# Output copies and the single tokens' first splits in the second MLP of a fused attention and MLP kernel

## The chip, the cores and the metric

The kernel runs on one core of one Trainium2 chip. The metric is the device time of one launch in microseconds (us). Before the change it is 966.17 us, the median of three runs that lie between 964.99 and 968.43 us. TensorE (PE) multiplies matrices, VectorE (DVE) and ScalarE (ACT) do elementwise work, GpSimd (POOL) hardly works here, and SyncE (SP) issues the DMAs.

## What is computed

A windowed attention with global tokens gives 2304 tokens of 512 features. They go through a gated MLP (512 to 1536 to 512) and then through a second MLP (512 to 2048 to 512) with a leaky ReLU. The change touches the second MLP alone.

```python
x = np.ascontiguousarray(attn_out.transpose(0, 2, 1, 3)).reshape(B * S, H * D)   # 2304 x 512
x = _moe_ref(x=x, **moe_kwargs)          # first MLP, 512 -> 1536 -> 512
h = x @ w_in                             # second MLP, 512 -> 2048
g = np.maximum(0.01 * h, h)
out = (g @ w_out).astype(np.float32)     # 2048 -> 512
```

All of it is float32. Each operand of a matrix product is split into a high part in the fast format fp32r (a cast on ACT, `high`, line 82) and a low part, the rest (a subtraction on DVE, `low`, line 85). A product is then three matmuls (`mm3`, line 78): high by high, one operand's low by the other's high, and the reverse. So a matmul has to wait for ACT's cast and then for DVE's subtraction.

## The kernel before

The attention runs ahead of and beside the first MLP. The second MLP follows as a section of its own at the end (functions `up`, `dn`, `out_tile` and the `rest_` functions, and one loop over g that calls them). Its order is written out by hand: on PE, DVE, ACT and SP each engine does its work in the order in which the code is written, so an instruction that waits holds up everything behind it on its engine.

The 2304 tokens of the second MLP are two blocks of 1024 tokens (s = 0 and 1) and 128 single tokens (REST). A block goes through 16 steps, numbered g: eight steps `up` (j = 0 to 7) make the hidden values, a pair of 128-wide columns each, and eight steps `dn` multiply them by `w_out`. So g = 0 to 7 and 8 to 15 are block 0, g = 16 to 23 and 24 to 31 block 1. PAIRS is 8.

- `up(g)` forms its hidden values from seven products of sums of blocks instead of eight (the tokens' sums are `ysa` and `ysb`, the weights' sums `wr`). PE's products in order are px, pw, py, pz into four PSUM banks, then a second px, py and pz on top of the first. Between a bank's two products the first result is read: ACT copies px into `x1`, DVE adds `u2 = x1 + pw`, `v = u2 + py`, `h[3] = v + pz`. Only then may PE add the second py onto py (line 1084) and the second pz onto pz. `x1`, `u2` and `v` are three SBUF buffers of 128 by 512, one each, and every step takes the same three again.
- The hidden values of pair j lie in a buffer of its own with tag `h0` to `h7`, 128 by 4 by 512. `dn` splits them into high and low (`dop_of`), four pieces a pair, some steps ahead.
- The weights' sums `wr` of block 0 are made in the kernel (`make_w` with place 0, 1 and 2, one step ahead: two casts on ACT of 128x768 and 128x1024, two subtractions on DVE of the same shapes, and at place 2 also the load of a later pair's weights, `load_q`). They are stored in DRAM by `keep_parts`, and block 1 loads them from there (`fetch_w`, line 929, 1792 KB each). There are two `wr` buffers, so the load for a step can start when PE has done the step before last.
- The single tokens are worked through beside the 16 `up` steps, two units a step: `rest_pair(u)` splits the weights of two units on ACT and DVE and issues the loads of the next two (two `raw` buffers, line 984), `rest_step(u)` is a unit's three matmuls (pr for the first layer, po for the second). Before the first of them `rest_second` splits the tokens themselves (`yr`). In step 0 these come at the end of `up`, in later steps earlier.
- In the last `dn` step of a block (j = 7) PE finishes the eight output tiles one after the other, six matmuls each. `out_tile` copies a tile from PSUM to an SBUF buffer `ob` (DVE and ACT in turn) and SP stores it to DRAM (line 973). The buffers are those of `x1`, `u2` and `v`, tile t in the place t modulo 3.

Of the kernel before, what the change touches and what calls it, by code (L numbers as in the profile page):

```python
# [8 lines left out]
F32 = mybir.dt.float32  # L9
# [7 lines left out]
P = 128  # L17
# [7 lines left out]
def tile_window_global_attention_two_mlps(  # L25
# [12 lines left out]
    _, _, KB, NT, _ = v_b.shape  # L38
# [6 lines left out]
    DM = NP * P  # L45
# [35 lines left out]
    def high(hi, src):  # L81
        nc.scalar.copy(hi, src)  # L82

    def low(lo, src, hi):
        nc.vector.tensor_tensor(out=lo, in0=src, in1=hi.bitcast(F32), op=ALU.subtract)  # L85

    def split(hi, lo, src):
        high(hi, src)
        low(lo, src, hi)
# [44 lines left out]
    def bank(name, early=False):  # L134

        return pools[0].tile([P, 512], F32, tag="y" if early else "b", bufs=pools[1], name=name)
# [486 lines left out]
    PAIRS = NF2 // 2  # L623
# [43 lines left out]
    def weight_sums(q):  # L667

        a21, a22, a11, a12, s1, s2, s3, s4 = (q[:, s] for s in range(8))
        for dst, x, y, op in ((s1, a21, a22, ALU.add), (s2, s1, a11, ALU.subtract),  # L670
                              (s3, a11, a21, ALU.subtract), (s4, a12, s2, ALU.subtract)):
            nc.vector.tensor_tensor(out=dst, in0=x, in1=y, op=op)
# [5 lines left out]
    def weight_parts(j):  # L678

        t = w_in[0, j] = ring(j)  # L680
        return [(t[:, 0, r], t[:, 1, r], slice(r.start + 1, r.stop + 1)) for r in (slice(0, 3), slice(3, 7))]

    def keep_parts(j):
        nc.sync.dma_start(out=w2_dram[j], in_=w_in[0, j].bitcast(F32).rearrange("p y s c -> p y (s c)"))
# [4 lines left out]
    def load_q(j):  # L689

        if j < PAIRS:
            q = wq[j] = quarter() if j % 2 else rings[1].tile([P, 8, HK], F32, tag=f"h{PAIRS - 1}", name=f"q{j}")
            for s, f in ((0, j + PAIRS), (2, j)):
                nc.sync.dma_start(out=q[:, s:s + 2].rearrange("p s c -> p (s c)"), in_=w2_f32[f][0])
# [203 lines left out]
    wp2 = ctx.enter_context(tc.tile_pool(name="wp2", bufs=1, reuse_waits="tile"))  # L898
# [13 lines left out]
    def kind(g):  # L912
        s, r = divmod(g, 2 * PAIRS)
        return (s, *divmod(r, PAIRS))

    def fetch_w(g):

        if g >= NU:
            return
        s, layer, j = kind(g)  # L920
        if layer:
            t = ring(g).rearrange("p y s c -> p (y s c)")
            raw = wfs[g] = t[:, 4 * DM:6 * DM].bitcast(F32).rearrange("p (f c) -> p f c", f=2)
            w_out[g] = t[:, 0:4 * DM].rearrange("p (y f c) -> p y f c", y=2, f=2)
            for x, f in enumerate((j, j + PAIRS)):
                nc.sync.dma_start(out=raw[:, x], in_=w2_f32[f][1])
        elif s:
            t = w_in[s, j] = ring(g)
            nc.sync.dma_start(out=t.bitcast(F32).rearrange("p y s c -> p y (s c)"), in_=w2_dram[j])

    def make_w(g, place):

        if g >= NU:
            return
        s, layer, j = kind(g)
        if layer:
            if place == 0:
                high(w_out[g][:, 0], wfs[g])
            elif place == 1:
                low(w_out[g][:, 1], wfs[g], w_out[g][:, 0])  # L940
        elif s == 0:
            q = wq[j]
            if place == 0:
                wq["parts"] = weight_parts(j)
                high(wq["parts"][0][0], q[:, wq["parts"][0][2]])
                weight_sums(q)
            elif place == 1:
                low(wq["parts"][0][1], q[:, wq["parts"][0][2]], wq["parts"][0][0])
                high(wq["parts"][1][0], q[:, wq["parts"][1][2]])
            else:  # L950
                low(wq["parts"][1][1], q[:, wq["parts"][1][2]], wq["parts"][1][0])
                load_q(j + 2)
# [5 lines left out]
    def product(s, j, which, dst, start=True):  # L958
        w, part, x = PRODUCT[which]
        t, y = w_in[s, j], ys2[s, part]  # L960
        for k in range(KC // 2):
            mm3(dst, [t[:, h, w, k * P:(k + 1) * P] for h in range(2)], [y[:, h, k, x] for h in range(2)],
                start and k == 0, k == KC // 2 - 1, not start)

    def plus(out, x, y):
        nc.vector.tensor_tensor(out=out, in0=x, in1=y, op=ALU.add)

    def leaky(out, x):
        nc.scalar.activation(out=out, in_=x, func=AF.Prelu, alpha=0.01)

    def store_rows(c0, ob):
        for r0, o, m in rows(c0, P):
            nc.sync.dma_start(out=out[r0:r0 + m, :], in_=ob[o:o + m, :])
# [5 lines left out]
    def rest_load(u):  # L979

        raw = rest["raw", u] = wp2.tile([P, HALF], F32, tag="raw", bufs=2, name=f"raw{u}")
        if u < NRU:
            fq, kc = divmod(u, KC)
            nc.sync.dma_start(out=raw.rearrange("p (f c) -> p f c", c=P), in_=w2_fours[fq][:, :, kc * P:(kc + 1) * P])
        else:
            nc.sync.dma_start(out=raw, in_=w2_f32[u - NRU][1])

    def rest_split(u):

        t = rest["w", u] = halves_tile(f"rw{u}")  # L990
        split(t[:, 0], t[:, 1], rest.pop(("raw", u)))
        if u >= NRU and u % 4 == 0:
            t = rest["h"] = wp2.tile([P, 2, 4, P], F32R, tag="yr", name=f"hr{u}")
            split(t[:, 0], t[:, 1], rest["hid"][:, u - NRU:u - NRU + 4])

    def rest_pair(u):
        for x in (u, u + 1):
            rest_split(x)
        for x in (u + 2, u + 3):
            if x < NRU + NF2:  # L1000
                rest_load(x)

    def rest_first():
        rest["y32"] = wp2.tile([P, HALF], F32, tag="hn", name="yr32")
        nc.sync.dma_start(out=rest["y32"].rearrange("p (k c) -> p k c", k=KC), in_=y_dram[:, :, 0:REST])

    def rest_second():
        rest["y"] = wp2.tile([P, 2, KC, P], F32R, tag="yr", name="yr")
        split(*(rest["y"][:, h].rearrange("p k c -> p (k c)") for h in range(2)), rest["y32"])
        rest["hid"] = wp2.tile([P, NF2, P], F32, tag="hid", name="hid")  # L1010
# [33 lines left out]
    def dop_of(s, x):  # L1044

        if x < 4 * PAIRS:
            j, r = divmod(x, 4)
            f, n = SLOTS[r]
            t = dops[s, x] = halves_tile(f"d{s}_{x}")
            split(t[:, 0], t[:, 1], hid[s, j][:, 2 * n + f])  # L1050

    def up(g):
        s, _, j = kind(g)
        u = 2 * (s * PAIRS + j)
        if g == 0:
            rest_first()
            rest_load(0)
            rest_load(1)
            load_q(2)
        if (s, j) != (1, 0):  # L1060
            fetch_w(g + 1)
        if s == 0 and j:
            keep_parts(j)
        h = hid[s, j] = wp2.tile([P, 4, HALF], F32, tag=f"h{j}", name=f"h{s}_{j}")
        x1, u2, v = [wp2.tile([P, HALF], F32, tag=x, name=f"{x}{s}_{j}") for x in ("x1", "u2", "v")]
        bx, bw, by = [bank(f"p{c}{s}_{j}") for c in "xwy"]
        product(s, j, 1, bx)
        nc.scalar.copy(x1, bx)
        product(s, j, 6, bw)
        plus(u2, x1, bw)  # L1070
        if g:
            rest_pair(u)
        product(s, j, 7, by)
        plus(v, u2, by)
        make_w(g + 1, 0)
        bz = bank(f"pz{s}_{j}")
        product(s, j, 5, bz)
        plus(h[:, 3], v, bz)
        make_w(g + 1, 1)
        product(s, j, 2, bx, False)  # L1080
        leaky(h[:, 0], bx)
        if j == PAIRS - 1:
            dop_of(s, 0)
            dop_of(s, 1)
        product(s, j, 4, by, False)
        plus(h[:, 1], u2, by)
        make_w(g + 1, 2)
        if g:
            rest_step(u)
        product(s, j, 3, bz, False)  # L1090
        plus(h[:, 2], u2, bz)
        leaky(h[:, 1:4], h[:, 1:4])
        if j == PAIRS - 1:
            dop_of(s, 2)
        if not g:
            rest_second()
            rest_pair(u)
            rest_step(u)
        rest_step(u + 1)

    def out_tile(s, t, last):
        ob = wp2.tile([P, DM], F32, tag=("x1", "u2", "v")[t % 3], name=f"ob{s}_{t}")
        if last % 2:
            nc.vector.tensor_copy(ob, dn.op[t])
        else:
            nc.scalar.copy(ob, dn.op[t])
        store_rows(REST + 2 * HALF * s + t * P, ob)
# [102 lines left out]
```

## Time and profile before

| | before |
|---|---|
| median of three runs | 966.17 us (964.99 to 968.43) |
| the profiled execution, its own time | 969.37 us |
| its span, first to last instruction | 967.6 us |
| granted TensorE clock, mean (1 is 2.4 GHz) | 0.985 |
| busy: PE, DVE, ACT | 927.2 us (96%), 585.6 us (61%), 461.1 us (48%) |
| chain that ended last, by engine | PE 72%, DMA 7%, DVE 3%, ACT 2% |
| of it, DMA of `ob` to the output | 2% |

The busy share of an engine is a mean over all stages. The chain that ended last is followed back from the last instruction, at each step to what released it, and so shows which waits count. The timeline gives each instruction with its start, its duration and, in brackets, how long its engine stood idle before it and what ended that. In the second MLP, from about 597 us on, PE is busy nearly without a gap but in two places, near 608 us and near 788 us.

### The profile page before, as it was taken

The numbers are of one execution on the slowest core, as the hardware profiler recorded it, in microseconds if no ns is written. First come the engines' busy times: TensorE is split into PE (matmuls) and PEld (weight loads), VectorE is DVE, ScalarE is ACT, GpSimd is POOL, SyncE is SP. The second block draws the span as 40 slices with busy tenths as digits, with TensorE's granted clock in tenths as the row PEclk, the third lists the DMA queues.
The fourth block names the chain that finished last, engine by engine and source line by source line (L and its number), as shares of the span: only waits on it lengthen the run. The fifth ranks groups of instructions, "written<-read, shape, count | busy, mean of one in ns | idle before, by whom it ended". The sixth has DMA issues, their size and how long they took to land.

```text
span 967.6 us, 14064 instructions
## 1 busy us (share of the span) xinstructions
PE 927.2 (96%) x5056; PEld 759.4 (78%) x5056; DVE 585.6 (61%) x1216; ACT 461.1 (48%) x958; POOL 4.5 (0%) x26
## 2 busy tenths in 40 slices
PE   6799999999999999999999999899999969999998
PEld 4557777777777777777899999688888858888886
DVE  5689985597676887444577744577665224445332
ACT  6886774655554555333454422445544213434331
POOL 1000000000000000000000000000000000000000
PEclk9899999999999999999999999999999979999999
DMA  9588994886769999744789982576333355651113
GB/s 305 172 284 264 313 354 150 273 286 226 253 215 380 346 367 343 260 131 142 283 282 338 362 296 79 200 276 246 142 93 104 94 188 196 225 189 54 44 47 107
DMA packets 87174, 215.37 MB, mean 223 GB/s; under 512 B 11456, under 2 KB 25280, under 8 KB 85056
## 3 DMA queue, kind: packets, MB, share of 16 engines
q1 hardware_dynamic: 87104, 214.47, 64.3%
q8 instruction: 40, 0.66, 0.3%
q14 instruction: 30, 0.25, 0.1%
HBM read 154.14 MB, written 60.29 MB: 222 GB/s over the span
## 4 chain that ended last, share of the span: by engine, by line
PE 72%; DMA 7%; DVE 3%; ACT 2%; issue 1%; SPq 0%; DVEq 0%; ACTq 0%
PE o L78 17%; PE pg L78 10%; PE yp L78 10%; PE pv L78 10%; PE py L78 5%; PE px L78 4%; PE pz L78 4%; DMA q<-y_dram 2%; PE pw L78 2%; PE po L146 2%; DMA out<-ob 2%; PE sc L146 2%; DMA y_dram<-ys 2%; PE pp L255 1%; PE pr L78 1%; PE po L78 1%
## 5 line engine op out<-in xcount | busy, mean ns | idle before, releaser
L78 PE MATMUL o<-wr,d 128*128 128x512 f32 x768 | 174.4, 390 | 0.0
L78 PEld LDWEIGHTS o<-wr,d 128*128 128x128 f32 x768 | 144.3, 188 | 29.8
L78 PE MATMUL pg<-xh,w 128*128 128x512 f32 (+1 forms) x464 | 132.6, 368 | 0.4 <-ACT xh L82 0.4
L78 PE MATMUL pv<-xh,w 128*128 128x512 f32 (+1 forms) x464 | 129.6, 361 | 0.0
L78 PE MATMUL yp<-hsh,w 128*128 128x512 f32 (+1 forms) x480 | 124.7, 365 | 2.7 <-ACT hsh L82 1.8
L78 PEld LDWEIGHTS yp<-hsh,w 128*128 128x128 f32 x480 | 84.0, 188 | 16.3 <-ACT hsh L82 2.8
L78 PEld LDWEIGHTS pg<-xh,w 128*128 128x128 f32 x464 | 80.8, 188 | 17.6 <-issue 5.8
L78 PEld LDWEIGHTS pv<-xh,w 128*128 128x128 f32 x464 | 82.3, 188 | 11.4 <-issue 1.3
L78 PE MATMUL pg<-xl,w 128*128 128x512 f32 (+1 forms) x232 | 83.3, 359 | 0.0
L78 PE MATMUL pv<-xl,w 128*128 128x512 f32 (+1 forms) x232 | 83.1, 358 | 0.0
L78 PE MATMUL yp<-hsl,w 128*128 128x512 f32 (+1 forms) x240 | 75.4, 362 | 0.1
L82 ACT CAST w<-wf 128x512 fp32r<-128x512 f32 x92 | 56.6, 616 | 38.3 <-PE yp L78 19.2
L235 ACT ACTIVATE s_ring<-s_ring,mx 128x224 f32<-128x224 f32 x128 | 60.3, 473 | 29.4 <-DVE mx L232 29.0
L85 DVE TENSOR_TENSOR w<-wf,w 128x512 fp32r<-128x512 f32 x92 | 63.0, 686 | 15.1 <-ACT w L82 14.2
L85 DVE TENSOR_TENSOR d<-h,d 128x512 fp32r<-128x512 f32 x64 | 42.0, 688 | 34.2 <-ACT d L82 34.2
L82 ACT CAST hsh<-th 128x512 fp32r<-128x512 f32 (+1 forms) x60 | 33.4, 556 | 55.6 <-DVE th L836 54.8
L82 ACT CAST d<-h 128x512 fp32r<-128x512 f32 x64 | 38.4, 619 | 37.5 <-PE o L78 37.5
L836 DVE SCALAR_TENSOR_TENSOR th<-th,pv 128x512 f32<-128x512 f32 (+1 forms) x60 | 36.3, 605 | 29.3 <-PE pv L78 28.7
L78 PE MATMUL pz<-ysb,wr 128*128 128x512 f32 x192 | 49.6, 394 | 0.0
L78 PEld LDWEIGHTS yp<-hsl,w 128*128 128x128 f32 x240 | 43.8, 188 | 6.5 <-DVE hsl L85 0.3
L78 PEld LDWEIGHTS pg<-xl,w 128*128 128x128 f32 x232 | 43.6, 188 | 6.6 <-DVE xl L85 0.3
L78 PEld LDWEIGHTS pv<-xl,w 128*128 128x128 f32 x232 | 43.6, 188 | 5.3
(160 smaller groups left out, 1431.6 us busy)
## 6 DMA issues: line engine op xcount, KB each, us to landing
w<-w_dram SPq DMA_DIRECT2D x84, 512.0 KB, 5.8
w<-w SPq DMA_DIRECT2D x36, 512.0 KB, 5.8
w_dram<-w SPq DMA_DIRECT2D x36, 512.0 KB, 4.2
w64b<-w SPq DMA_DIRECT2D x32, 512.0 KB, 6.5
wf<-w_f SPq DMA_DIRECT2D x60, 256.0 KB, 4.7
w_dram<-wr SPq DMA_DIRECT2D x8, 1792.0 KB, 8.2
wr<-w_dram SPq DMA_DIRECT2D x8, 1792.0 KB, 7.4
kq<-kqv SPq DMA_DIRECT2D x32, 352.0 KB, 5.5
```

The lines of the kernel that those rows point to most:

```text
L78: nc.tensor.matmul(dst, lhs[a], rhs[b], start=first and i == 0, stop=last and i == 2, skip_group_check=onto)
L82: nc.scalar.copy(hi, src)
L85: nc.vector.tensor_tensor(out=lo, in0=src, in1=hi.bitcast(F32), op=ALU.subtract)
L146: x = nc.tensor.matmul(dst, lhs, rhs, start=start, stop=stop)
L235: x = nc.scalar.activation(out=sp, in_=sp, func=AF.Exp, bias=mx[:, c:c + 1], scale=-1.0, accum_out=sm[:, c:c + 1])
L255: nc.tensor.transpose(pp[:, n * P:(n + 1) * P], s[:, c0:c0 + P], ident)
L836: nc.vector.scalar_tensor_tensor(out=t, in0=t, scalar=0.5, in1=pp[1][:, 0:n], op0=ALU.mult, op1=ALU.mult)
```

## The change

It makes two edits in the second MLP.

The first moves two calls in step 0. `rest_second()` and `rest_pair(0)`, which stood behind the step's last products, now stand in front of `make_w(1, 2)`, the subtraction for the second part of the next step's weights and the load behind it. The matmuls of unit 0 and 1 stay where they were.

The second takes other buffers for the output copies. Tiles 0 to 3 (in the order in which they are copied) go into one buffer of 128 by 4 by 512 in the place of `h5`, tiles 4 to 7 into one in the place of `h6`. No buffer is added.

```diff
@@ up(g)
         product(s, j, 4, by, False)
         plus(h[:, 1], u2, by)
+        if not g:
+            rest_second()
+            rest_pair(u)
         make_w(g + 1, 2)
         if g:
             rest_step(u)
@@
         if j == PAIRS - 1:
             dop_of(s, 2)
         if not g:
-            rest_second()
-            rest_pair(u)
             rest_step(u)
         rest_step(u + 1)
 
     def out_tile(s, t, last):
-        ob = wp2.tile([P, DM], F32, tag=("x1", "u2", "v")[t % 3], name=f"ob{s}_{t}")
+        if last % 4 == 0:
+            dn.ob = wp2.tile([P, 4, DM], F32, tag=f"h{PAIRS - 3 + last // 4}", name=f"ob{s}_{last}")
+        ob = dn.ob[:, last % 4]
```

The place on DVE is the second half of step 0. The rows with line 85 are subtractions, `wr` the weights' sums, `yr` the single tokens, `rw` the weights of a unit; in brackets stands what a row waits for (a queue of the DMAs, or an engine).

```order
 L966 TENSOR_TENSOR h_0_6415<-u_0_6417,py_0_6421 128x512 [waits PE_49]
-L85 TENSOR_TENSOR wr_6443<-q,wr_6443 128x1024 [waits Activation_49]
+L85 TENSOR_TENSOR yr<-yr_6406,yr 128x512 [waits DMAHW4_49,Activation_49]
+L85 TENSOR_TENSOR rw_6477<-raw_6408,rw_6477 128x512 [waits DMAHW5_49,Activation_49]
+L85 TENSOR_TENSOR rw_6480<-raw_6410,rw_6480 128x512 [waits DMAHW6_49,Activation_49]
+L85 TENSOR_TENSOR wr_6443<-q,wr_6443 128x1024 [waits DVE_49]
 L966 TENSOR_TENSOR h_0_6415<-u_0_6417,pz_0_6449 128x512 [waits PE_49]
-L85 TENSOR_TENSOR yr<-yr_6406,yr 128x512 [waits DMAHW4_49,Activation_49]
-L85 TENSOR_TENSOR rw_6489<-raw_6408,rw_6489 128x512 [waits DMAHW5_49,Activation_49]
-L85 TENSOR_TENSOR rw_6492<-raw_6410,rw_6492 128x512 [waits DMAHW6_49,Activation_49]
```

The three subtractions of the single tokens now stand ahead of the weights' long one and of the addition that waits for the second pz. On ACT, in the same place, the casts move in the same way ahead of the long leaky ReLU (128x1536).

```order
 L969 ACTIVATE h_0_6415<-px_0_6419 128x512 [waits PE_49]
+L82 CAST yr<-yr_6406 128x512 [waits DMAHW4_49]
+L82 CAST rw_6477<-raw_6408 128x512 [waits DMAHW5_49]
+L82 CAST rw_6480<-raw_6410 128x512 [waits DMAHW6_49]
 L969 ACTIVATE h_0_6415<-h_0_6415 128x1536 [waits DVE_49]
-L82 CAST yr<-yr_6406 128x512 [waits DMAHW4_49]
-L82 CAST rw_6489<-raw_6408 128x512 [waits DMAHW5_49]
-L82 CAST rw_6492<-raw_6410 128x512 [waits DMAHW6_49]
 L1068 COPY x_1_6508<-px_1_6511 128x512 [waits PE_49,Activation_49]
```

That leaky ReLU now stands directly ahead of the copy of `x1` in step 1. On SP the loads of units 2 and 3 (`raw`) change places with those of the pair 3 weights (`q`):

```order
 L694 DMA q_6412<-w_fours_100 128x512 [waits DMAHW0_49]
-L694 DMA q<-w_fours_102 128x512 [waits DMAHW1_49,DVE_49]
-L694 DMA q<-w_fours_100 128x512 [waits DMAHW2_49]
-L984 DMA raw_6495<-w_fours_100 128x4x128 [waits DMAHW5_49,DMAHW3_49,DVE_49]
-L984 DMA raw_6497<-w_fours_100 128x4x128 [waits DMAHW6_49,DMAHW4_49,DVE_49]
+L984 DMA raw_6483<-w_fours_100 128x4x128 [waits DMAHW5_49,DMAHW1_49,DVE_49]
+L984 DMA raw_6485<-w_fours_100 128x4x128 [waits DMAHW6_49,DMAHW2_49,DVE_49]
+L694 DMA q<-w_fours_102 128x512 [waits DMAHW3_49,DVE_49]
+L694 DMA q<-w_fours_100 128x512 [waits DMAHW4_49]
 L684 DMA w_dram_121<-wr_6443 128x3584
```

The store of the weights' sums (`w_dram`) stays behind both. The other place is DVE at the seam of the two blocks, where it copies tiles 1, 3, 5 and 7 of block 0 and then begins step 16. Before the change:

```order
L1104 COPY ob0_1_7677<-o0_1_7144 128x512 [waits PE_49]
L1104 COPY ob0_3_7695<-o0_3_7146 128x512 [waits DMAHW3_49,PE_49,Activation_49]
L1104 COPY ob0_5_7713<-o0_5_7148 128x512 [waits DMAHW5_49,PE_49,Activation_49]
L1104 COPY ob0_7_7733<-o0_7_7150 128x512 [waits DMAHW4_49,DMAHW7_49,PE_49,Activation_49]
L966 TENSOR_TENSOR u21_0_7738<-x11_0_7737,pw1_0_7741 128x512 [waits DVE_49,DMAHW3_49,PE_49,Activation_49]
```

With the change:

```order
L1107 COPY ob0_0_7668<-o0_1_7144 128x512 [waits PE_49]
L1107 COPY ob0_0_7668<-o0_3_7146 128x512 [waits PE_49]
L1107 COPY ob0_4_7701<-o0_5_7148 128x512 [waits DVE_49,PE_49]
L1107 COPY ob0_4_7701<-o0_7_7150 128x512 [waits PE_49]
L966 TENSOR_TENSOR u21_0_7732<-x11_0_7731,pw1_0_7735 128x512 [waits PE_49,Activation_49]
```

The copies and the addition of `u2` (u21 here: block 1, pair 0) have lost their waits for the stores. The number and the kind of the instructions are the same on every engine.

## Rows read from the trace of the kernel before

**Rows 1.** The page: busy time, span share and instructions of each engine.

```profile
PE 927.2 (96%) x5056; PEld 759.4 (78%) x5056; DVE 585.6 (61%) x1216; ACT 461.1 (48%) x958; POOL 4.5 (0%) x26
```

**Rows 2.** Timeline, step 0: start us, us, engine line op out<-in xcount [idle before <-releaser].

```profile
599.35 1.29 SPq L984 DMA_DIRECT2D raw<-w_fours  x2
...
604.13 0.59 ACT L969 ACTIVATE h<-px 128x512 f32<-128x512 f32 x1
...
604.87 1.52 PE L78 MATMUL pz<-ysb,wr 128*128 128x512 f32 x6
605.07 0.69 DVE L966 TENSOR_TENSOR h<-u,py 128x512 f32<-128x512 f32 x1 [0.46 <-PE py L78]
605.67 1.22 DVE L85 TENSOR_TENSOR wr<-q,wr 128x1024 fp32r<-128x1024 f32 x1
...
607.52 1.48 ACT L969 ACTIVATE h<-h 128x1536 f32<-128x1536 f32 x1 [2.80 <-DVE h L966]
608.91 0.60 ACT L82 CAST yr<-yr 128x512 fp32r<-128x512 f32 x1
609.42 1.14 ACT L82 CAST rw<-raw 128x512 fp32r<-128x512 f32 x2
...
610.09 2.87 PE L78 MATMUL pr<-rw,yr 128*128 128x512 f32 x6 [3.70 <-ACT rw L82]
610.15 1.29 DVE L85 TENSOR_TENSOR rw<-raw,rw 128x512 fp32r<-128x512 f32 x2
...
614.87 1.52 PE L78 MATMUL pw<-ysa,wr 128*128 128x512 f32 x6
```

**Rows 3.** The tile raw, 598 to 614 us: time from issue to landing.

```profile
DMA to landing us min/median/max: 3.1/3.4/4.0
```

**Rows 4.** Chain that ended last, steps 2 and 3: start us, us, what.

```profile
624.55 1.36 PE px L78 x6
...
635.92 1.36 PE px L78 x6
```

**Rows 5.** Chain that ended last, at the seam of the two blocks.

```profile
769.46 7.99 DMA out<-ob
...
781.99 7.70 DMA out<-ob
```

**Rows 6.** Timeline, the seam of the two blocks.

```profile
767.48 0.32 SPq L929 DMA_DIRECT2D wr<-w_dram  x1
...
778.17 1.52 PE L78 MATMUL px<-ysa,wr 128*128 128x512 f32 x6
...
783.32 0.58 ACT L1068 COPY x<-px 128x512 f32<-128x512 f32 x1 [2.25 <-DMA out<-ob]
...
789.81 0.69 DVE L966 TENSOR_TENSOR u<-x,pw 128x512 f32<-128x512 f32 x1 [7.98 <-DMA out<-ob]
...
792.95 2.93 PE L78 MATMUL py<-ysb,wr 128*128 128x512 f32 x6 [7.35 <-DVE v L966]
...
800.30 1.52 PE L78 MATMUL px<-ysa,wr 128*128 128x512 f32 x6
```

**Rows 7.** DMA issues, 767.4 to 767.6 us: xcount, KB each, us to landing.

```profile
wr<-w_dram SPq DMA_DIRECT2D x1, 1792.0 KB, 9.5
```

**Rows 8.** DMA issues, 781.45 to 781.6 us, the next such load.

```profile
wr<-w_dram SPq DMA_DIRECT2D x1, 1792.0 KB, 7.5
```

**Rows 9.** DMA issues, 781.0 to 781.15 us, a store of an output tile.

```profile
out<-ob SPq DMA_DIRECT2D x1, 256.0 KB, 2.1
```

**Rows 10.** DMA packets by size, 773.5 to 774 us and 774.5 to 775 us.

```profile
DMA packets 10, 0.14 MB, mean 287 GB/s; under 512 B 0, under 2 KB 0, under 8 KB 0
...
DMA packets 83, 0.17 MB, mean 340 GB/s; under 512 B 12, under 2 KB 12, under 8 KB 81
```

**Rows 11.** Busy time by stretch: us, PE, PEld, DVE, ACT, POOL busy (x), PEclk, DMA share, GB/s.

```profile
803.00:963.00 160.00, 160.00 (x707) 132.63 (x706) 66.00 (x95) 55.27 (x82) 0.00 (x0) 1.00 0.36 122
```

**Rows 12.** Chain that ended last, its end.

```profile
929.89 33.79 PE o L78 x149
```

## The prediction

> **What bounds the kernel now.** I read the page first, then the chain that ended last, then the timeline at the places where the chain leaves PE. PE is busy 96% of the span [rows 1], so there is little left but its gaps, and in the second MLP the chain leaves PE at two places only. One is the end of step 0: PE begins the single tokens' matmuls (pr) at 610.09 after 3.70 us of idle time, put down to ACT's cast of `rw` [rows 2]. The other is the seam of the two blocks: the chain goes through two stores of output tiles of 7.99 and 7.70 us [rows 5], and PE begins the second py of step 16 at 792.95 after 7.35 us, put down to DVE's `v` [rows 6]. Both are waits for an order or a buffer, not for a lack of an engine's time. The end of the program is PE's: 149 matmuls without a break until the last copy [rows 12]; what saves time earlier therefore comes off the end one for one, as long as nothing else becomes late.
>
> **Edit 1, the single tokens in step 0.** What it takes away: DVE's subtractions for `yr`, `rw` 0 and `rw` 1 stood behind the 128x1024 subtraction (1.22 us), the addition that waits for the second pz, and ACT's long leaky ReLU (1.48 us) that waits for that addition [rows 2]. The work itself stays. I rebuild the stretch from the durations:
>
> - ACT is free at 604.13 + 0.59 = 604.72. The cast pitch is 609.42 - 608.91 = 0.51 us, so `yr`, `rw` 0 and `rw` 1 are cast by about 605.3, 605.8 and 606.3 [rows 2]. Their inputs are there: the second of their two loads is issued by 600.64 and takes at most 4.0 us, 604.6, a microsecond before its cast [rows 2, 3].
> - DVE starts `h` at 605.07; back to back its pitch is 605.67 - 605.07 = 0.60 us. `yr` starts at 605.67, `rw` 0 at 606.27 and ends near 606.96, `rw` 1 ends near 607.56. The 128x1024 subtraction then ends near 608.7 and the addition near 609.3 [rows 2].
> - PE ends the second pz at 604.87 + 1.36 = 606.23 (six matmuls take 1.36 us, 0.227 each [rows 4]). The first two pr matmuls follow at once, the third waits for `rw` 0 until 607.0, and the six end at about 607.9. Step 1's px takes 1.36 us, so its pw begins at 609.27. It needs the second part of the weights, ready at 608.7.
>
> Before, that pw began at 614.87 [rows 2], with matmuls that ran slowly just after the idle time. So edit 1 gives 614.87 - 609.27 = **5.6 us**. Its bounds: nothing, if a new wait eats it all, and 5.9 us, if no wait is left at all (606.23 + 2.72 = 608.95). I take 5.6, since every duration in it has its row.
>
> What is late next: the `x1` copy of step 1 now stands behind the long leaky ReLU, which must wait for the addition (609.3) and ends at 610.8; `x1` ends near 611.4, `u2` near 612.0, two subtractions later `v` near 613.9. PE wants `x1` for its second px at 607.9 + 4 x 1.36 = 613.4 and `v` for its second py at 614.7: covered, by 0.8 us at the tightest. On SP the loads of units 2 and 3 now go ahead of pair 3's weights. They are issued when their buffers are free, near 607.0 and 607.6, and land by 611.6 at 4.0 us [rows 3], as their cast comes up (611.4). The two loads of pair 3 and the store of the sums move from a wait behind other work to about 608.7, and pair 3 is used two steps later, so this costs nothing.
>
> **Edit 2, the output copies.** What it takes away is the wait of the copies of tiles 3 to 7, and of `x1`, `u2` and `v` in step 16, for the stores of earlier tiles, with 2.25 us before `x1` and 7.98 before `u2` [rows 6]. These are not added up, since they partly lie beside PE's work; PE itself is the measure. From its px of step 16 to that of step 17 it takes 800.30 - 778.17 = 22.13 us [rows 6]. A step with the same products, two units and a turn of the hidden values (pt) takes 635.92 - 624.55 = 11.37 us [rows 4]. Step 16 begins when it began before, because the last output tiles ended PE's work there, not a copy. So edit 2 gives 22.13 - 11.37 = **10.8 us**, the slow matmuls after the gap among them (2.93 us for six, against 1.36). It can't give more; the least is nothing, if another wait takes the place.
>
> Does step 16 then flow? The copies come at PE's pace of 1.36 us a tile and the last one ends at about 779.1, ahead of `u2`, which needs pw (780.9). Then `u2`, three subtractions and `v` at 0.60 us each end near 784.1; PE wants `v` at 778.17 + 5 x 1.36 = 785.0. Covered by 0.9 us. The old readers of `h5` and `h6` are long done at the seam, and the next writers come five steps later, so the new place makes no wait. The end of the program keeps its length: there the copies already followed PE.
>
> The DMAs are what is late next. Eight stores are now issued at 1.36 us intervals between the load of step 16's weights (767.48) and that of step 17's, which SP issues when PE has left the buffer, at 778.3. The first load took 9.5 us and landed at 777.0, 1.2 us before PE asked for it [rows 6, 7]. In the half microsecond from 773.5 no packet under 8 KB was served, though a store had been waiting since 769.46; from 774.5 on nearly all packets were such ones [rows 5, 10]. So the stores wait behind the load, and five more of them do not delay it. The Trainium skill ("DMA: Bandwidth & Descriptors", section "Queues, rings and completion order") says both that one engine's DMAs lie in one row, taken in ring order, and that a DMA engine serves several rows in turn, a packet from each. By the first the load is not delayed and the sum stays as it is; by the second it would be, which is the third rival below. The packet rows speak for the first.
>
> The same order puts the load of step 17's weights behind up to four stores. A store's 0.26 MB at the 340 GB/s of those rows takes 0.77 us [rows 10], so with 7.5 us of its own [rows 8] the load lands at 778.3 + 7.5 + 4 x 0.77 = 788.9 at the latest. PE wants it at 778.17 + 11.37 = 789.5. Covered, by 0.6 us at the worst, and by 2 to 3 us as some of the stores are served before 778.3.
>
> **The sum.** 5.6 + 10.8 = 16.4 us. The profiled execution took 969.37 us, so it would take 953.0. It lies 3.2 us above the median of the runs shown, so for the median I forecast 966.17 - 16.4 = **949.8 us**.
>
> **Rivals.**
>
> 1. *Edit 1's wait only moves.* A load of units 2 and 3 lands late, or ACT's `x1` copy does, and PE waits at the second px or py of step 1. For it: the cover is 0.8 us, and ACT takes `x1` in order behind a leaky ReLU that it did not have to wait for before. Against it: the rebuilt times. If all 5.6 us come back: 955.4 us. Chance 0.08.
> 2. *The load of step 17's weights is late.* For it: the stores ahead of it. If four of them each held it up by 2.1 us, a store's whole time at an idle queue [rows 9], it would land 7.5 + 8.4 us after 778.3, at 794.2, and PE would wait 4.7 us: 954.5. Against it: the rows have them served at 0.77 us. Chance 0.08.
> 3. *Stores and load share the engines.* Then the load of step 16's weights lands up to three stores later, 777.0 + 3 x 0.77 = 779.3, and PE waits 1.1 us: 950.9. The packet rows speak against it. Chance 0.05.
> 4. *The output copies still wait* for something that the order of the instructions does not show, and only edit 1 pays: 960.6. The waits for the stores are gone from the instructions, so 0.02.
> 5. *Slower.* With both gaps gone PE works from about 608 to 948 without a pause, 340 us. The longest such stretch before is 160 us, at a granted clock of 1.00 throughout [rows 11]. If the chip then granted the lower of its two levels (1.2 instead of 2.4 GHz) for part of the second block, each us of PE's work there would cost one more. From 16.4 us of such work on the gain is gone; 30 us would give 979.8. Nothing in the rows points to it: 0.02.
>
> **How the numbers follow.** The forecast has what is left, 0.75. The runs shown lie from 1.2 below their median to 2.3 above it. The gain cannot pass 5.9 + 10.8 = 16.7, and 966.17 - 16.7 - 1.2 is 948.3; the lower end is 947, for a little that the rebuilt times don't know. Upwards the range takes in rivals 1 to 3 and ends at 956. Left out are rivals 4 and 5 and the tails of the others, some 0.1. A measurement of this kernel can tell about 0.3% (2.9 us) from no change. All cases but the fifth are faster by more than that: 0.97 faster, 0.01 within it, 0.02 slower.
>
> **What would show it.** Right: pr of step 0 starts right behind the second pz, with under 1 us of idle time in all, and step 1's pw some 3 us behind the end of pz, instead of 8.6; ob copies that wait for PE alone, 1.36 us apart; the px of steps 16 and 17 some 11.4 us apart; no `out<-ob` in the chain before the end; no low clock in the second MLP. Wrong: a wait of PE for `v` in step 1 (rival 1), for the weights' load in step 17 (rival 2) or 16 (rival 3), a store in the chain at the seam (rival 4), a granted clock under 1 in a dense stretch (rival 5). A gain of under 11 us would mean that one of the two sums is wrong.

## The result and the profile after

The changed kernel takes 951.96 us, the median of four runs (951.21 to 953.81), against 967.09 us for four runs of the kernel before. The ratio is 0.9848 with a 95% interval of 0.9824 to 0.9873, which is 14.7 us less (12.3 to 17.0); the two medians are 15.1 us apart. The forecast was 949.8 us and 16.4 us less, the range 947 to 956.

One number ahead of the prediction is to be set right: the attention gives 4 times 544, that is 2176 tokens (two blocks of 1024 and 128 single ones), not 2304. No time and no sum hangs on it.

The page of the changed kernel, its busy times, which answer to [rows 1], and the chain by engine:

```profile
span 949.4 us, 14049 instructions
...
PE 922.1 (97%) x5056; PEld 756.0 (80%) x5056; DVE 585.3 (62%) x1216; ACT 461.1 (49%) x958; POOL 4.5 (0%) x26
...
PE 79%; DMA 5%; DVE 3%; ACT 2%; issue 1%; SPq 1%; DVEq 0%; ACTq 0%
```

The work is the same. PE's busy time falls by only 5.1 us; the rest was idle time. It falls mostly because matmuls behind the two gaps ran at the lower level of the clock. Two stretches of the kernel before, busy time and, third from the end, the granted clock:

```profile
611.00:614.00 3.00, 3.00 (x7) 2.39 (x8) 0.44 (x1) 0.00 (x0) 0.00 (x0) 0.50 0.54 158
793.00:798.00 5.00, 5.00 (x14) 4.04 (x15) 1.37 (x2) 0.00 (x0) 0.00 (x0) 0.50 0.24 70
```

The clock was 0.50 there (1.2 GHz), just behind 3.70 and 7.35 us of idle time on PE; with the change it is 1.00 at both places. The chain's share on PE rises from 72% to 79%.

The timeline of step 0, which answers to [rows 2]:

```profile
603.00 1.52 PE L78 MATMUL pz<-ysb,wr 128*128 128x512 f32 x6
...
603.27 1.14 ACT L82 CAST rw<-raw 128x512 fp32r<-128x512 f32 x2
603.81 0.69 DVE L85 TENSOR_TENSOR yr<-yr,yr 128x512 fp32r<-128x512 f32 x1
604.36 1.98 PE L78 MATMUL pr<-rw,yr 128*128 128x512 f32 x6
604.41 1.29 DVE L85 TENSOR_TENSOR rw<-raw,rw 128x512 fp32r<-128x512 f32 x2
605.12 1.21 SPq L984 DMA_DIRECT2D raw<-w_fours  x2
605.61 1.22 DVE L85 TENSOR_TENSOR wr<-q,wr 128x1024 fp32r<-128x1024 f32 x1
...
607.54 1.52 PE L78 MATMUL pw<-ysa,wr 128*128 128x512 f32 x6
...
611.27 0.68 DVE L966 TENSOR_TENSOR v<-u,py 128x512 f32<-128x512 f32 x1
...
612.98 1.52 PE L78 MATMUL py<-ysb,wr 128*128 128x512 f32 x6
```

The single tokens' matmuls (pr) start right behind the second pz and no bracket stands at them any more, where 3.70 us stood before. (From pr to the next px it is 1.82 us, not the 1.36 of six matmuls without a wait, so about 0.5 us of waiting is left inside the group.) Step 1's `v` ends at 611.95, 1.0 us ahead of PE's second py.

The timeline at the seam, which answers to [rows 6]:

```profile
760.15 0.32 SPq L929 DMA_DIRECT2D wr<-w_dram  x1
...
765.60 0.69 DVE L1107 COPY ob<-o 128x512 f32<-128x512 f32 x1 [2.03 <-PE o L78]
766.96 0.59 ACT L1109 COPY ob<-o 128x512 f32<-128x512 f32 x1 [2.13 <-PE o L78]
...
770.84 1.52 PE L78 MATMUL px<-ysa,wr 128*128 128x512 f32 x6
771.03 0.33 SPq L929 DMA_DIRECT2D wr<-w_dram  x1
...
776.24 0.68 DVE L966 TENSOR_TENSOR v<-u,py 128x512 f32<-128x512 f32 x1
...
777.64 1.52 PE L78 MATMUL py<-ysb,wr 128*128 128x512 f32 x6
...
782.20 1.53 PE L78 MATMUL px<-ysa,wr 128*128 128x512 f32 x6
```

The copies follow PE at 1.36 us a tile and wait for PE alone. The second py has no wait. From the px of step 16 to that of step 17 it takes 11.36 us.

Two spacings of PE's matmuls measure the edits without the noise of what lies ahead: **S1**, from the second pz of step 0 to the pw of step 1, and **S2**, from the px of step 16 to that of step 17. The table has them for every kernel, with the start of the second MLP's first px (P), the stretch from that pw to the px of step 16 (M) and the stretch from the px of step 17 to the end of the last instruction (E), all in us and from the profiled execution of each kernel. S1, M and S2 are differences of two starts in its timeline; P counts from the start of the span, and E is what is left of the span, which the page gives to 0.1 us.

| kernel | P | S1 | M | S2 | E | span |
|---|---|---|---|---|---|---|
| before | 596.68 | 10.00 | 163.30 | 22.13 | 167.30 | 967.6 |
| the change | 594.82 | 4.54 | 163.30 | 11.36 | 167.20 | 949.4 |
| edit 1 alone | 597.60 | 4.57 | 163.31 | 21.42 | 167.31 | 962.4 |
| edit 2 alone | 597.36 | 9.91 | 163.32 | 11.36 | 167.26 | 957.4 |
| splits behind the low | 594.37 | 5.70 | 163.31 | 11.36 | 167.27 | 950.2 |
| loads behind | 594.81 | 4.53 | 165.73 | 11.36 | 167.19 | 951.8 |
| three places | 600.76 | 4.58 | 163.31 | 12.15 | 167.31 | 956.3 |
| last three back | 600.18 | 4.58 | 163.31 | 20.21 | 167.23 | 963.7 |
| store first | 597.90 | 9.41 | 163.32 | 14.25 | 167.33 | 960.4 |
| stores from ACT | 599.37 | 4.54 | 163.30 | 11.36 | 167.25 | 954.0 |

The change takes 5.46 us out of S1, 10.77 out of S2 and 0.1 out of E, 16.3 in all. Of the 5.46 us, 3.86 lie between the second pz and pr, the gap itself, and 1.60 behind it, in matmuls at the lower clock. Of the 10.77, 7.98 lie ahead of the second py and 2.79 behind its start. So over a quarter of the gain is not the gaps but the slow matmuls that followed them. The spans differ by 18.2; the other 1.9 us lie ahead of the second MLP (P). P goes from 594.4 to 600.8 us in these ten executions, though no edit touches what stands there: that is the noise of the total times, and the spacings are free of it: M is 163.30 to 163.32 and S2 is 11.36 in every kernel in which nothing there was touched. The two kernels with splits or loads moved back, the one with the last three copies back and the one with the stores from ACT were executed once each, so only their spacings are read.

### The profile page after: what moved, and what is told of

It reads as the page before. It is cut to its first block, busy times and chain, and to the rows that moved or that the text cites. A ratio compares the mean times of both kernels' runs of the same rounds, so it can differ in the third digit from the quotient of the medians.

```text
span 949.4 us, 14049 instructions
## 1 busy us (share of the span) xinstructions
PE 922.1 (97%) x5056; PEld 756.0 (80%) x5056; DVE 585.3 (62%) x1216; ACT 461.1 (49%) x958; POOL 4.5 (0%) x26
## 4 chain that ended last, share of the span: by engine, by line
PE 79%; DMA 5%; DVE 3%; ACT 2%; issue 1%; SPq 1%; DVEq 0%; ACTq 0%
PE o L78 18%; PE pg L78 12%; PE yp L78 12%; PE pv L78 11%; PE pz L78 4%; PE px L78 4%; PE py L78 4%; PE po L146 3%; PE sc L146 2%; PE pw L78 2%; DMA q<-y_dram 2%; DMA y_dram<-ys 2%; PE pp L255 2%; PE po L78 1%; PE pr L78 1%
## 5 line engine op out<-in xcount | busy, mean ns | idle before, releaser
L85 DVE TENSOR_TENSOR w<-wf,w 128x512 fp32r<-128x512 f32 x92 | 62.9, 684 | 15.1 <-ACT w L82 14.2
L832 DVE SCALAR_TENSOR_TENSOR th<-th,pg 128x512 f32<-128x512 f32 (+1 forms) x58 | 34.7, 598 | 21.4 <-ACT th L831 21.0
```

The costliest lines, as they stand in the source:

```text
L832: x = nc.vector.scalar_tensor_tensor(out=t, in0=t, scalar=1.0, in1=gate, op0=ALU.add, op1=ALU.mult)
```

## The experiments

### Each edit alone

Edit 1 alone keeps the copies in `x1`, `u2` and `v`:

```diff
-        if last % 4 == 0:
-            dn.ob = wp2.tile([P, 4, DM], F32, tag=f"h{PAIRS - 3 + last // 4}", name=f"ob{s}_{last}")
-        ob = dn.ob[:, last % 4]
+        ob = wp2.tile([P, DM], F32, tag=("x1", "u2", "v")[t % 3], name=f"ob{s}_{t}")
```

> Edit 1 alone; the output copies use x1, u2 and v as before the change. Two spacings of PE's matmuls measure the two edits apart from the noise of the first MLP: S1, from the second pz of step 0 to the pw of step 1 (10.00 us before, 4.54 with the change), and S2, from the first px of step 16 to that of step 17 (22.13 before, 11.36 with the change). Theory (the two stalls are independent): S1 4.5 and S2 22.1 us, the time 5.5 us under before (ratio 0.994). Rival (the seam stall depends on what came before it, through the DMA queue or the clock): S2 differs from 22.1 by over 1 us.

Measured: S1 4.57, S2 21.42, ratio 0.9931 (0.9908 to 0.9955), which is 6.7 us less than the 967.79 us of before (4.4 to 8.9); the two medians are 4.6 us apart, the spacings together 6.1.

Edit 2 alone leaves the calls in step 0 at its end:

```diff
-        if not g:
-            rest_second()
-            rest_pair(u)
         make_w(g + 1, 2)
...
         if not g:
+            rest_second()
+            rest_pair(u)
             rest_step(u)
```

> Edit 2 alone; the single tokens' splits stand where they stood. Theory (independent stalls): S1 10.0 and S2 11.4 us, the time 10.8 us under before (ratio 0.989). Rival (edit 2 needs edit 1, or gives something elsewhere too, such as at the end of the program): S2 over 12.4 us, or the stretch from the px of step 17 to the last instruction differs from 167.3 us by over 0.5.

Measured: S1 9.91, S2 11.36, E 167.26, ratio 0.9899 (0.9881 to 0.9918), 9.8 us less (7.9 to 11.5). The two edits are independent to within 0.7 us: each takes out its own spacing and leaves the other one and the rest of the program. S2 with edit 1 alone is 0.7 us shorter than before, less than the 1 us that the rival needed. A spacing with a gap in it differs from one execution to the next: S1 is 10.00, 9.91 and 9.41 in the three kernels that have the old step 0. The gap is the same in all three (from pz to pr 5.22, 5.22 and 5.21 us); what differs is how long the matmuls behind it took (from pr to pw 4.78, 4.69 and 4.20 us). Of the 0.7 us of S2, 0.57 lie ahead of the second py. Whether edit 1 has a part in that is not shown, with one execution of each.

### Which place in the queue counts in step 0

The splits come one subtraction later, behind `make_w(1, 2)`, on top of the change:

```diff
-        if not g:
-            rest_second()
-            rest_pair(u)
         make_w(g + 1, 2)
+        if not g:
+            rest_second()
+            rest_pair(u)
```

> The changed kernel, but the single tokens' splits stand behind the weights' last subtraction (128x1024) and pair 3's loads, still ahead of the addition and the leaky ReLU. Theory (the DVE queue sets when the single tokens' matmuls can go, so each subtraction in front counts with its pitch): the three subtractions start 1.1 us later, the third matmul waits until about 1.9 us behind the end of pz, S1 5.5 us (1.0 more than with the change). Rival (the stall came from the addition and the leaky ReLU alone, the 1.22 us subtraction is free): S1 4.5. Rival (a place behind the subtraction brings most of the old stall back): S1 over 8.

Measured: S1 5.70 us, 1.16 more than with the change. The timeline of this kernel at that place:

```profile
603.36 1.22 DVE L85 TENSOR_TENSOR wr<-q,wr 128x1024 fp32r<-128x1024 f32 x1
603.91 0.39 PE L78 MATMUL pr<-rw,yr 128*128 128x512 f32 x1
604.50 0.68 DVE L85 TENSOR_TENSOR yr<-yr,yr 128x512 fp32r<-128x512 f32 x1
...
605.24 1.80 PE L78 MATMUL pr<-rw,yr 128*128 128x512 f32 x5 [0.93 <-DVE yr L85]
605.81 1.20 SPq L984 DMA_DIRECT2D raw<-w_fours  x2
```

The first matmul (high by high) goes, the second waits 0.93 us for the subtraction of `yr`, which stands behind the long one. (The theory had the wait at the third matmul.) So DVE's queue sets the time, by the pitch of what stands in front (1.14 us from `wr` to `yr`). Of the 5.46 us of edit 1, 4.3 come from passing the addition and the leaky ReLU, and 1.2 from passing the subtraction as well.

Then the loads alone go back behind pair 3's loads on SP, the splits stay in front:

```diff
         if not g:
             rest_second()
-            rest_pair(u)
+            rest_split(u)
+            rest_split(u + 1)
         make_w(g + 1, 2)
+        if not g:
+            rest_load(u + 2)
+            rest_load(u + 3)
```

> The changed kernel, but the loads of units 2 and 3 stay behind the loads of pair 3's weights on SP; only the splits move. Theory (SP works in order and these loads are needed half a microsecond after they land): S1 stays at 4.5 us, the loads are issued some 2.5 us later, their subtractions and so v of step 1 come later, and PE waits for v before its second py: the px of step 1 to that of step 2 takes 11.3 to 11.9 us instead of 10.88. Rival (the order on SP is covered): 10.9 us.

Measured: S1 4.53, and from the px of step 1 to that of step 2 13.31 us instead of 10.88 (it shows in M). The theory has the direction and the place, but the cost is 2.43 us, where it gave 0.4 to 1.0. Timeline of this kernel:

```profile
605.60 1.22 DVE L85 TENSOR_TENSOR wr<-q,wr 128x1024 fp32r<-128x1024 f32 x1
...
606.88 0.80 SPq L694 DMA_DIRECT2D q<-w_fours  x2
...
607.79 1.20 SPq L984 DMA_DIRECT2D raw<-w_fours  x2
...
612.44 0.62 ACT L82 CAST rw<-raw 128x512 fp32r<-128x512 f32 x1 [3.03 <-DMA raw<-w_fours]
...
615.23 1.66 PE L78 MATMUL py<-ysb,wr 128*128 128x512 f32 x6 [2.10 <-DVE v L966]
```

And the same tile's loads in the DMA line of its view:

```profile
DMA to landing us min/median/max: 4.6/4.7/4.8
```

I had taken 3.2 us from issue to landing; behind the two loads of pair 3 it took 4.7, and ACT and DVE both stood waiting for it in order, so that `v` came 2.1 us later than PE wanted it. The larger part of the delay is the issue: these loads went out at 607.79 instead of 605.12, since the load of pair 3 in front of them on SP had to wait for the weights' subtraction (it ends at 606.82 in this kernel). In the run with the splits behind the subtraction, the same loads stood behind those of pair 3 as well, but that subtraction came early; they went out at 605.81, landed in 3.6 to 4.5 us, and M did not move. So it is not the place behind another load alone that costs, but what that load waits for. The move of the loads on SP, which the diff shows only as part of `rest_pair`, is thus worth 2.4 us of the total: without it nearly half of edit 1 is given back one step later, which is the first rival of the prediction.

### What held the seam: the copies' waits or step 16's buffers

Three places in rotation for the copies, which step 16 does not use:

```diff
-        if last % 4 == 0:
-            dn.ob = wp2.tile([P, 4, DM], F32, tag=f"h{PAIRS - 3 + last // 4}", name=f"ob{s}_{last}")
-        ob = dn.ob[:, last % 4]
+        ob = wp2.tile([P, 4, DM], F32, tag=f"h{PAIRS - 3 + last % 3}", name=f"ob{s}_{t}")[:, 0]
```

> The changed kernel with three places for the output copies in rotation (those of h5, h6 and h7) instead of eight; x1, u2 and v stay free of copies. So copies 3 to 7 wait for stores again, as before the change, but step 16's own buffers don't. Theory (what cost the time was that x1, u2 and v were held, the copies' own waits were beside PE's work): copies 3 to 7 start near where they did before the change, S2 11.4 to 12.4 us, within 1 us of the change. Rival (the copies' waits hold up ACT, DVE and SP in front of step 16, and that is a large part): S2 14 us or more.

Measured: S2 12.15, ratio 0.9857 (0.9817 to 0.9897). Timeline of this kernel:

```profile
776.98 0.69 DVE L1105 COPY ob<-o 128x512 f32<-128x512 f32 x1 [7.41 <-DMA out<-ob]
777.58 0.59 ACT L1107 COPY ob<-o 128x512 f32<-128x512 f32 x1 [6.75 <-DMA out<-ob]
...
784.29 1.66 PE L78 MATMUL py<-ysb,wr 128*128 128x512 f32 x6 [0.49 <-DVE v L966]
```

The same two copies before the change:

```profile
777.57 0.69 DVE L1104 COPY ob<-o 128x512 f32<-128x512 f32 x1 [6.67 <-DMA out<-ob]
778.17 0.59 ACT L1106 COPY ob<-o 128x512 f32<-128x512 f32 x1 [6.01 <-DMA out<-ob]
```

The copies wait for stores even longer than before the change, 7.41 and 6.75 us, and it costs 0.79 us of S2. So nearly all of edit 2's gain comes from the buffers that it sets free for step 16, not from the copies' own waits.

The other way round, the last three copies go back into `v`, `x1` and `u2`:

```diff
+        if last < 5:
+            if last % 4 == 0:
+                dn.ob = wp2.tile([P, 4, DM], F32, tag=f"h{PAIRS - 3 + last // 4}", name=f"ob{s}_{last}")
+            ob = dn.ob[:, last % 4]
+        else:
+            ob = wp2.tile([P, DM], F32, tag=("x1", "u2", "v")[t % 3], name=f"ob{s}_{t}")
```

> The changed kernel, but copies 5, 6 and 7 go into v, x1 and u2 again, copies 0 to 4 stay in the places of h5 and h6. No copy waits for a store; step 16's buffers are held by the last three stores. Theory (the hold on x1, u2 and v is what costs, above all u2 by the last store, which is queued behind step 17's weights): that store lands some 9.5 us after its issue, u2 starts then, PE's second py stands idle for 6 to 7 us, S2 20 to 21 us. Rival (the copies' waits were the cost): S2 11.4.

Measured: S2 20.21. No copy waits for a store, and 8.85 of the 10.77 us are gone again:

```profile
786.87 0.69 DVE L966 TENSOR_TENSOR u<-x,pw 128x512 f32<-128x512 f32 x1 [9.72 <-DMA out<-ob]
...
790.02 2.92 PE L78 MATMUL py<-ysb,wr 128*128 128x512 f32 x6 [6.80 <-DVE v L966]
```

The last store was issued at 777.18 and took 9.6 us, behind step 17's weights; `u2` waited for it, and PE for `v`.

The third one leaves the buffers of before and exchanges two DMAs on SP:

```diff
-                if n == NT2 - 1 and s + 1 < NS:
-                    fetch_w(g + 2)
                 out_tile(s, t, n)
+                if n == NT2 - 1 and s + 1 < NS:
+                    fetch_w(g + 2)
```

> The kernel before, with one exchange on SP: the last store of block 0 is issued ahead of step 17's weights instead of behind them. Copies and buffers as before the change. Theory (DMAs of SP are served in the order of issue, so 5.6 of that store's 7.70 us were the 1792 KB load in front of it): the store lands in 2.1 us, u2 starts near 6 us earlier, S2 13 to 15 us, the time 7 to 9 us under before. Rival (all DMAs in flight share the engines): the store takes 4 us or more, S2 16 or more.

Measured: the last store lands in 2.1 us, S2 is 14.25, the ratio 0.991 (0.9877 to 0.9942), 8.7 us less than 967.77 (5.6 to 11.9). Timeline of this kernel, and its DMA issues from 782.9 to 783.2 us:

```profile
784.98 1.65 PE L78 MATMUL px<-ysb,wr 128*128 128x512 f32 x6 [0.55 <-ACT x L1068]
785.23 0.69 DVE L966 TENSOR_TENSOR u<-x,pw 128x512 f32<-128x512 f32 x1 [2.29 <-DMA out<-ob]
...
788.38 1.66 PE L78 MATMUL py<-ysb,wr 128*128 128x512 f32 x6 [1.75 <-DVE v L966]
```

```profile
out<-ob SPq DMA_DIRECT2D x1, 256.0 KB, 2.1
```

This exchange of two lines alone gives 7.9 of the 10.8 us: most of the old stall was one small store queued behind one large load. It leaves 2.3 us of idle time on PE (0.55 and 1.75), which edit 2's buffers take away. In this run the copies come late and the three buffers are still shared; which of the two makes the 2.9 us that are left of S2 is not taken apart by a run.

### Who is served first

The stores are issued by ACT, in another queue than the loads:

```diff
-            nc.sync.dma_start(out=out[r0:r0 + m, :], in_=ob[o:o + m, :])
+            nc.scalar.dma_start(out=out[r0:r0 + m, :], in_=ob[o:o + m, :])
```

> The changed kernel, but the stores of the output are issued by ACT instead of SP, so that they are in another queue than the weights' loads. Theory A (the DMA engines serve queues in turn, and only DMAs of one queue in the order of issue): the first store lands 2 to 5 us after its issue instead of 7.5, the load of step 16's weights takes 10 to 12.5 us instead of 8.8, and PE waits up to 2 us for it at the seam. Theory B (order of issue, whatever the queue): the first store takes 7 to 8 us, the load 8.8.

Measured: the first store takes 7.0 us and the load beside it 8.5, and PE does not wait (M 163.30, S2 11.36). Queues on the page of this kernel, and the DMA issues of 764.7 to 764.8 us and of 766.6 to 766.8 us:

```profile
q1 hardware_dynamic: 84608, 210.01, 63.5%
q10 hardware_dynamic: 2496, 4.46, 1.3%
```

```profile
wr<-w_dram SPq DMA_DIRECT2D x1, 1792.0 KB, 8.5
...
out<-ob ACTq DMA_DIRECT2D x1, 256.0 KB, 7.0
```

DMA packets by size in the same kernel, from 769 to 770, from 770 to 771 and from 771 to 772 us:

```profile
DMA packets 29, 0.42 MB, mean 416 GB/s; under 512 B 0, under 2 KB 0, under 8 KB 0
...
DMA packets 17, 0.22 MB, mean 221 GB/s; under 512 B 0, under 2 KB 0, under 8 KB 2
...
DMA packets 107, 0.25 MB, mean 246 GB/s; under 512 B 17, under 2 KB 17, under 8 KB 102
```

The stores are in a queue of their own (q10) and still wait: the first was issued at 766.68, and hardly a small packet is served before 771, when the load's large ones are all but through. The last store, issued less than 1 us behind step 17's load, took 8.9 us. That is theory B, for a small store behind one large load.

## Why the prediction was right, point by point

- **Edit 1.** 5.6 us forecast, 5.46 measured. The rebuilt queue held: pw of step 1 was to come 4.40 us after the second pz, it came after 4.54. The 0.14 us are in the pr matmuls: from pr to the end of the six it was to be 1.67 us (607.9 - 606.23), it was 1.82. The subtraction of `wr` in front is priced by its pitch, as the run with the splits behind it shows.
- **Its cover.** `v` was to be done 0.8 us ahead of PE and was 1.0 ahead. The landing of the loads of units 2 and 3 was forecast at 4.0 us at most; it was 3.1 and 3.3. The first rival did not come, but the run with the loads behind shows that it is real: there the same step costs 2.4 us.
- **Edit 2.** 10.8 us forecast, 10.77 measured; S2 is 11.36, a step in steady flow [rows 4] was 11.37. `v` of step 16 was to be done 0.9 us ahead of PE and was 0.7 ahead. The prediction took PE's spacing as the measure and did not add up the waits of the copies; the run with three places shows that these waits were worth 0.8 us. Which hold cost the time, the prediction left open; the runs name it: the three buffers of step 16, and above all the last store behind the load.
- **The loads of the weights.** The load of step 16's weights took 8.8 us beside the five stores that were issued while it ran, against 9.5 beside three [rows 7]: the third rival is out. The prediction tied it to several queues being served in turn, but stores and loads are all issued by SP here and lie in one queue (q1 on the page); a second queue came only with the run with the stores from ACT. The load of step 17's took 9.5 us and landed at 780.5, 1.7 us ahead of PE; the forecast had 0.6 at worst and 2 to 3 otherwise. The second rival did not come.

The DMA issues of the changed kernel, 760.1 to 760.3 us and 771.0 to 771.1 us:

```profile
wr<-w_dram SPq DMA_DIRECT2D x1, 1792.0 KB, 8.8
...
wr<-w_dram SPq DMA_DIRECT2D x1, 1792.0 KB, 9.5
```

- **The clock.** The fifth rival is out. Busy time by stretch, which answers to [rows 11]:

```profile
597.00:947.00 350.00, 348.47 (x1544) 287.82 (x1542) 178.58 (x271) 141.07 (x203) 0.00 (x0) 1.00 0.46 156
```

  PE works 348.5 of 350 us, at a granted clock of 1.00.
- **The sum.** 16.4 us forecast, 16.3 in the spacings, 14.7 (12.3 to 17.0) in the total times. The 949.8 us were too low by 2.2: 0.9 of it is the median of before, which stands at 967.09 with a fourth run instead of 966.17. The rest is smaller than the spread of the stages ahead of the second MLP and is not traced to a step.

## What to carry to other kernels

Where a copy borrows a buffer, look at who takes that buffer next and at what its release is queued behind: here one 256 KB store behind a 1792 KB load held an addition, and the addition held PE, while the copies' own waits, nearly as long in the trace, cost 0.8 us. Measure a stall by the spacing of the bounding engine's instructions around it, not by adding up waits on the others. When work is moved ahead in an in-order program, move the loads that it issues as well, and say in the sum what the load in front of them waits for and how long they will take to land: here they went out 2.7 us later and took 4.7 us instead of 3.2.

## What the runs showed of the hardware that was not expected

- A small store in ACT's queue waited behind a large load that SP had issued 2 us earlier (7.0 us to landing, 2.1 for the same store at an idle time [rows 9]). The rule of the Trainium skill that was weighed in the prediction ("DMA: Bandwidth & Descriptors", section "Queues, rings and completion order"), that a DMA engine serves several queues in turn by the packet, did not show here, but the run does not refute it either. A packet there is a group of descriptors, typically 9 to 17 of them. The load's queue had 144 packets of the profile while it ran (764.7 to 773.3 us), about nine for each of the 16 DMA engines; if an engine takes them as one packet of the rule, the rule too lets the load go first. Whether that is so, or something else orders them, was not tried.
- A short gap on PE costs little beside itself, a long one more. In the run with the store first, six matmuls after 1.75 us of idle time were busy for 1.66 us (1.52 in steady flow), at a granted clock of 1.00; in the one with the last three copies back they took 2.92 us after 6.80 us, at 0.50. S2 exceeds 11.36 by 2.89 us for 2.30 us of idle time in the first, and by 8.85 for 6.80 in the second.
